# One PSUM bank for the recurrence's gradient chain, three for the scores, in a woven backward pass

## The chip, the cores and the metric

The kernel runs on one core of a Trainium2 chip. The core has five engines that run their own instruction streams in order and wait for one another through semaphores: TensorE (matmuls, PE in the profile; its weight loads are listed as PEld), VectorE (DVE), ScalarE (ACT), GpSimd (POOL) and SyncE (SP), which here issues most of the DMA transfers. Matmuls write to PSUM, which has eight banks of 2 KB per partition; a 128x512 float32 tile fills one bank. The time is that of one execution on the device, in microseconds (us); the median of five runs of the kernel before is 6302.86 us (6299.35 to 6306.31).

## What is computed

The reference computes a gated mix of two attention blocks and then all gradients of it. The output is `g * a + (1 - g) * b`; `jax.vjp` gives the gradients for eleven inputs. Cut to what matters here:

```python
def _A_ref(x, wq, wk, wv, wo):            # 32 query heads of 18, one key and value head
    q = (x @ wq).reshape(B, S, H, Dh).transpose(0, 2, 1, 3)
    k, v = x @ wk, x @ wv
    p = softmax(einsum('bhqd,bkd->bhqk', q, k) * Dh ** -0.5)
    return einsum('bhqk,bkd->bhqd', p, v) ... @ wo

def _B_ref(x, mem0, Wq, Wk, Wv, Wo, seg_len):   # 32 heads of 128
    mem = mem0                                   # 8 memory rows
    for s in range(n_seg):                       # 64 segments of 32 tokens
        h = concatenate([mem, x[:, s*32:(s+1)*32, :]], axis=1)
        q, k, v = (einsum('btd,dhe->bhte', h, W) for W in (Wq, Wk, Wv))
        p = softmax(where(mask, q k^T * scale, -1e9))
        o = einsum('bhte,hed->btd', p @ v, Wo)
        mem = o[:, :8, :]                        # the next segment needs it
        outs.append(o[:, 8:, :])
```

There are 2048 tokens of width 576. Block A is wide and has no order of its own. Block B is a recurrence: in the backward pass the gradient of a segment's eight memory rows is needed before the segment ahead of it can be done, so its 64 segments run one after another.

## The kernel before

The kernel is one program of several stages. The stage that the change touches is the backward weave. It interleaves two Python generators: `b_chain_bwd`, the chain, which carries the gradient of the memory rows from segment 63 down to 0, and `a_pass2`, the sweep, which recomputes block A's probabilities and accumulates the gradients of its keys and values. `weave` runs one piece of the chain (up to its next `yield`) and then one step of the sweep, over and over. The whole is built under a manual schedule: the instructions of an engine stand in the order in which the Python code issues them, so the order is written out by hand. Each segment has 16 pieces, and there are 64 x 16 = 1024 sweep steps.

**A sweep step n** (`a_pass2`) handles two heads for a block of 128 queries and 512 keys. On TensorE: `mm_S(n + 1)`, two score matmuls into the PSUM tile `b_S`; two matmuls into `b_dP` (a ring of three banks); four accumulating matmuls into `b_acc` for step n - 1, from `b_dS` and `b_E`. On ScalarE: `ex(n + 1)`, the exponential of `b_S` into the SBUF tile `b_E` (ring of three). On VectorE: two multiplies, `b_dS = b_dP * b_E`, one for each head. Every fourth step issues on SP the loads of `b_QD` and `b_SD` for the chunk after next (rings of three); the first step also issues `b_KV` and the first two chunks.

**A chain segment** goes through these pieces: the projection of the memory gradient `dm` by `WoT` (40 matmuls of 512 columns, `proj_part`), evacuated by ScalarE into `r_dOm`; its transposition `r_dOT` and the product `r_prod`; the gradient of the probabilities and `r_dS`; three memory gradients (`mem_grad` 2, 0 and 1), each copied by ScalarE into a part of `r_dT`, two of them after an expansion by GpSimd (`r_dSB`, `r_dSqB`); 48 units of `heads` (four matmuls of 288 columns each, against `WT`), 24 for each half of the 576 columns, each half then copied by ScalarE into `r_hs`; and `sums`, float32 matmuls that add up the heads' groups and from which VectorE writes the next `dm`. Along the way VectorE does three small transposes (`r_dsq`, `r_xq`, `r_pq`), and `load(s - 1)` issues the next segment's loads on SP: `r_vmT`, `r_vxT` (a DMA transpose), `r_pT`, `r_oT`, four `r_kx` and four `r_dx` in turn, `r_k` and `r_q`. `r_dx`, `r_k` and `r_q` are single buffers, so their loads wait for the memory gradients that read them. In the first segment `load_WT` issues six loads of `WT` on SP.

PSUM in this stage before the change: `r_pj` one bank (first half of the projection, and `heads`), `r_x` one bank (second half of the projection and all else of the chain), `b_S` two banks as one tile, `b_dP` three, `b_acc` one.

Of the kernel before, what the change touches and what calls it, by code (L numbers as in the profile page):

```python
# [6 lines left out]
ACT = mybir.ActivationFunctionType  # L7
# [3 lines left out]
F32 = mybir.dt.float32  # L11
P = 128

D = 576
NKT = 5
# [10 lines left out]
SCALEA = float(DA) ** -0.5  # L26
# [4 lines left out]
class Kern:  # L31
# [761 lines left out]
    def b_chain_bwd(self, keep, sp, psum):  # L793
        nc = self.nc
        NSEG = self.NSEG
# [9 lines left out]
        def load(s):  # L805
            L = {}
            L["vmT"] = sp.tile([P, HB, 8], BF16, name="r_vmT", bufs=2)
            nc.sync.dma_start(L["vmT"][:], self.mTd["v"][s])
            L["vxT"] = sp.tile([P, HB, 32], BF16, name="r_vxT", bufs=2)
            nc.sync.dma_start_transpose(L["vxT"][:], self.xtok["v"][s * 32:(s + 1) * 32, :])  # L810
            L["pT"] = sp.tile([P, 2, 64], BF16, name="r_pT", bufs=2)
            nc.sync.dma_start(L["pT"][:].rearrange("p a b -> p (a b)"), self.pm_dram[s])
            L["oT"] = sp.tile([P, 256], BF16, name="r_oT", bufs=2)
            nc.sync.dma_start(L["oT"][:], self.oTm_dram[s // 16][:, s % 16, :])
            L["kx"] = sp.tile([P, 8, E], BF16, name="r_kx", bufs=2)
            for c in range(4):
                nc.sync.dma_start(L["kx"][32 * c:32 * c + 32].rearrange("p u e -> p (u e)"),
                                  self.xtok["k"][s * 32:(s + 1) * 32, c * 1024:(c + 1) * 1024])
                nc.sync.dma_start(mrow["dx"][32 * c:32 * c + 8],
                                  self.dmx_dram[s * 8:s * 8 + 8, 8 * c:8 * c + 8].rearrange("m h w e -> m h (w e)"))  # L820
            for w in ("k", "q"):
                nc.sync.dma_start(mrow[w][:].rearrange("p u e -> p (u e)"), self.row_dram[w][s])
            return L
# [17 lines left out]
        for s in reversed(range(NSEG)):  # L841
            L = nxt
            d_ = dm[s % 2]
            pT = L["pT"]
            nc.gpsimd.dma_start(self.dmT_dram[:, :, s, :], d_[:, :, 0:8])
            dOm = sp.tile([P, 8, E], BF16, name="r_dOm", bufs=1)
            pj = [psum.tile([P, 512], F32, name=nm, bufs=1) for nm in ("r_pj", "r_x")]
            for k, parts in enumerate((((0, (0, 1, 2, 3)),), ((0, (4,)), (1, (0, 1))), ((1, (2, 3, 4)),))):
                for j, kts in parts:
                    self.proj_part(pj[j], d_, self.WoT, j, kts)  # L850
                    if kts[-1] == 4:
                        self.evac(dOm[:, 4 * j:4 * j + 4, :].rearrange("p u e -> p (u e)"), pj[j][:], use="s")
                if s == NSEG - 1 and k == 1:
                    self.load_WT()
                yield
            src = self.mem_T(dOm, psum, "r_x", 1)
# [29 lines left out]
            ph = {}  # L886
# [3 lines left out]
            def heads(n):  # L890
                for _ in range(n):
                    wi, hf, u = next(units)
                    if hf not in ph:
                        ph[hf] = psum.tile([P, 288], F32, name="r_pj", bufs=1)
                    for g in range(4):
                        self.mm(ph[hf][32 * g:32 * g + 32, :], lhsT=dT[:, wi, u, :],
                                rhs=self.WT[wi][:, 8 * g + u, 288 * hf:288 * hf + 288],
                                start=(wi == 2 and u == 0), stop=(wi == 1 and u == 7), tp=(0, 32 * g))
                    if wi == 1 and u == 7:
                        nc.scalar.copy(hs[:, 288 * hf:288 * hf + 288], ph[hf][:])  # L900

            def sums(kts):
                for kt in kts:
                    ncols = KT_ROWS[kt]
                    self.mm(pm[0:ncols, kt, :], lhsT=hs[:, kt * P:kt * P + ncols], rhs=self.selF[:, :])

            def mem_grad(wi, name, pairs):
                pg = psum.tile([P, 8, 32], F32, name=name, bufs=1)
                for u in range(8):
                    for n, (l, r) in enumerate(pairs):  # L910
                        self.mm(pg[:, u, :], lhsT=l[u], rhs=r[u], start=(n == 0), stop=(n == 1))
                nc.scalar.copy(dT[:, wi], pg[:])
# [6 lines left out]
            mem_grad(0, "r_x", ((rows(L["kx"]), blk(dSB)), (rows(mrow["k"]), blk(dSB, 8))))  # L919
            dSqB = sp.tile([P, 8, 4, 8], BF16, name="r_dSqB", bufs=1)  # L920
            self.expand(dSqB[:], dSq[:, 0, :, 0:8], 8)
            heads(4)
            yield
            heads(4)
            mem_grad(1, "r_x", ((rows(mrow["dx"]), [seln] * 8), (rows(mrow["q"]), blk(dSqB))))
            nc.gpsimd.dma_start(self.dTm_dram[s // 16][:, :, s % 16, :], dT[:].rearrange("p w u c -> p w (u c)"))
            if s:
                nxt = load(s - 1)
            yield
            heads(6)  # L930
            yield
            heads(6)
# [2 lines left out]
                nc.gpsimd.dma_start(self.pq_dram[s // 4, s % 4, :, c, :, 32 * (s % 4):32 * (s % 4) + 32],  # L935
                                    xq[32 * c:32 * c + 8].rearrange("p i u k -> p (i u) k"))
            yield
            heads(4)
            yield
            heads(6)  # L940
            yield
            heads(6)
            pm = psum.tile([P, NKT, 8], F32, name="r_x", bufs=1)
            sums((0, 1))
            yield
            heads(6)
            if s:
# [1 line left out]
            yield  # L949
            heads(6)  # L950
            yield
            sums((2, 3, 4))
            dn = dm[1 - s % 2]
            nc.vector.tensor_copy(dn[:, 0:4, 0:8], pm[:, 0:4, :])
            nc.vector.tensor_copy(dn[0:64, 4, 0:8], pm[0:64, 4, :])
# [554 lines left out]
    def a_pass2(self, keep, sp, psum):  # L1510
        nc = self.nc
        T, NTT = self.T, self.NTT
        KV = keep.tile([P, T], BF16, name="b_KV")
        nc.sync.dma_start(KV[:, :], self.kv_dram[:, :])
        Q, S, E_, D_ = {}, {}, {}, {}
        NC = 4 * NPR * NTT // 4

        def load(c):
            if c < NC:
                p, q4 = (c // 4) % NPR, c % 4  # L1520
                QD = sp.tile([P, 512], BF16, name="b_QD", bufs=3)
                nc.sync.dma_start(QD[:], self.qd_dram[p][:, q4 * 512:(q4 + 1) * 512])
                SD = sp.tile([P, 4, P], BF16, name="b_SD", bufs=3)
                nc.sync.dma_start(SD[:], self.sd_dram[p][:, 4 * q4:4 * q4 + 4, :])
                Q[c] = (QD, SD)

        def pair(n):
            return n // (NPR * NTT), n // 4, n % 4

        def mm_u(dst, n, base):  # L1530
            kb, c, j = pair(n)
            for i in range(2):
                r = slice(base + 32 * i, base + 32 * i + 32)
                self.mm(dst[i], lhsT=Q[c][0][r, j * P:j * P + P], rhs=KV[r, kb * 512:kb * 512 + 512],
                        tp=(base + 32 * i, 0))

        def mm_S(n):
            S[n] = psum.tile([P, 2, 512], F32, name="b_S", bufs=1)
            mm_u([S[n][:, i, :] for i in range(2)], n, 0)

        def ex(n):
            E_[n] = sp.tile([P, 2, 512], BF16, name="b_E", bufs=3)
            nc.scalar.activation(E_[n][:], S.pop(n)[:], ACT.Exp, scale=SCALEA)  # L1543

        load(0)
        load(1)
        mm_S(0)
        ex(0)
        acc = None
        NS = NPR * NTT  # L1550
        NP_ = 4 * NS
        for n in range(NP_ + 1):
            if n < NP_:
                if n % 4 == 2:
                    load(n // 4 + 2)
                if n + 1 < NP_:
                    mm_S(n + 1)
                dP = [psum.tile([P, 512], F32, name="b_dP", bufs=3) for _ in range(2)]
                mm_u([t[:] for t in dP], n, 64)
                if n + 1 < NP_:  # L1560
                    ex(n + 1)
                D_[n] = sp.tile([P, 2, 512], BF16, name="b_dS", bufs=2)
                for i in range(2):
                    nc.vector.tensor_tensor(out=D_[n][:, i, :], in0=dP[i][:], in1=E_[n][:, i, :], op=ALU.mult)  # L1564
            if n > 0:
                o = n - 1
                if o % NS == 0:
                    acc = psum.tile([P, 512], F32, name="b_acc", bufs=1)
                SD = Q[o // 4][1]
                src = (D_.pop(o), E_.pop(o))  # L1570
                for i4 in range(4):
                    self.mm(acc[32 * i4:32 * i4 + 32, :], lhsT=SD[:, o % 4, 32 * i4:32 * i4 + 32],
                            rhs=src[i4 // 2][:, i4 % 2, :],
                            start=(o % NS == 0), stop=(o % NS == NS - 1), tp=(0, 32 * i4))
                if o % NS == NS - 1:
                    dkv = sp.tile([P, 512], BF16, name="b_dkv", bufs=1)
                    nc.scalar.copy(dkv[:], acc[:])
                    k0 = (o // NS) * 512
                    nc.sync.dma_start(self.dkv_dram[:, k0:k0 + 512], dkv[:])
            yield  # L1580
# [229 lines left out]
```

The softmax here doesn't subtract the row's maximum and nothing guards it: scores larger than these inputs give would overflow.

## Time and profile before

| what | value |
|---|---|
| median of five runs | 6302.86 us |
| the profiled execution | 6302.93 us, span 6301.2 us |
| TensorE busy, share of the span | 5687.2 us, 90% |
| VectorE | 3753.6 us, 60% |
| ScalarE | 3483.2 us, 55% |
| GpSimd | 1952.0 us, 31% |
| the backward weave | first `b_S` matmul at 3198.57 us, last at 4863.90 us |

Times inside the profile are counted from the start of the span. "Busy" of an engine is the time in which at least one of its instructions runs; matmuls are pipelined, so a busy TensorE is not one at its peak. A group's line gives its source line, engine and operation, what it writes and reads, shapes and count; then its busy time and the mean duration in ns; then the idle time of the engine just before it and what ended most of that. Nearly all matmuls carry line 66, that of a helper, and are told apart by their tiles. In a timeline a line holds start, duration, engine, line, operation and count, in microseconds. The chain that ended last is followed backwards from the end of the program, from each instruction to what released it.

### The profile page before, as it was taken

The page shows a single profiled execution, that of the slowest core. Times are in us where ns is not written, and L with a number is a line of the kernel's source. Part 1 is how long each engine was busy: PE and PEld are TensorE (multiplying, and loading weights), DVE is VectorE, ACT ScalarE, POOL GpSimd, SP SyncE. Part 2 cuts the span into 40 slices and gives each one's busy share as a digit, 9 for nine tenths or more (in the row PEclk, how much of TensorE's full clock was granted, in tenths as well). Part 3 has the DMA queues.
Part 4 walks back from the last instruction along what each step waited for, and adds up shares of the span by engine and source line. Part 5 has one row for each costly group of instructions (what it writes and reads, how often), then busy time and mean ns, then how long its engine had stood idle before and what let it go on. Part 6 is the DMA issues. An engine that isn't in the chain of part 4 may idle for free.

```text
span 6301.2 us, 208815 instructions
## 1 busy us (share of the span) xinstructions
PE 5687.2 (90%) x88611; PEld 3382.1 (54%) x88822; DVE 3753.6 (60%) x7061; ACT 3483.2 (55%) x5105; POOL 1952.0 (31%) x3451
## 2 busy tenths in 40 slices
PE   7898999999999994999969999999998999899996
PEld 5443444444444443877735555555554777674443
DVE  4336777777777773666658888888887111121111
ACT  3326777777777773666647777777776222111101
POOL 3002333333333333444423333333333111122212
PEclk9999999999999997999989999999999999999998
DMA  4646666666665444999973444444343999896643
GB/s 153 227 150 114 121 120 122 122 124 120 121 123 108 99 86 140 256 258 257 257 223 108 109 112 109 107 107 107 109 108 102 248 239 244 246 259 198 221 149 113
DMA packets 1368110, 991.96 MB, mean 157 GB/s; under 512 B 931613, under 2 KB 1184806, under 8 KB 1356486
## 3 DMA queue, kind: packets, MB, share of 16 engines
q1 hardware_dynamic: 1285030, 780.53, 50.4%
q0 software_dynamic: 82144, 198.05, 10.0%
q8 instruction: 696, 11.40, 0.8%
q14 instruction: 240, 1.97, 0.1%
HBM read 552.41 MB, written 384.76 MB: 149 GB/s over the span
## 4 chain that ended last, share of the span: by engine, by line
PE 63%; ACT 18%; issue 8%; DMA 7%; SPq 3%; POOL 1%; DVE 1%; ACTq 0%; POOLq 0%; DVEq 0%
ACT b_E L1543 10%; PE w_acc L66 10%; PE c_pj L66 7%; PE a_acc L66 6%; PE b_S L66 6%; ACT a_E L1401 5%; PE a_S L66 5%; PE p_pb L66 4%; PE r_pj L66 4%; DMA dsx_dram<-x_dS 3%; PE r_x L66 2%; PE x_tr L71 2%; PE b_acc L66 2%; PE c_x L66 2%; PE y_pdx L66 2%
## 5 line engine op out<-in xcount | busy, mean ns | idle before, releaser
L1434 DVE TENSOR_TENSOR a_W<-a_dP,a_E 128x512 bf16<-128x512 f32 x2048 | 1315.6, 684 | 427.9 <-PE a_dP L66 365.6
L1564 DVE TENSOR_TENSOR b_dS<-b_dP,b_E 128x512 bf16<-128x512 f32 x2048 | 1313.2, 683 | 239.4 <-issue 120.0
L1543 ACT ACTIVATE b_E<-b_S 128x1024 bf16<-128x1024 f32 x1024 | 1047.8, 1023 | 445.5 <-PE b_dP L66 322.4
L1401 ACT ACTIVATE a_E<-a_S 128x1024 bf16<-128x1024 f32 x1024 | 1051.5, 1027 | 154.6 <-PE a_dP L66 139.4
L66 PE MATMUL b_S<-b_KV,b_QD 32*128 32x512 bf16 x2048 | 400.0, 381 | 157.0 <-ACT b_E L1543 101.3
L66 PE MATMUL r_pj<-WT,r_dT 128*32 128x288 bf16 x12288 | 492.2, 287 | 1.6 <-DMA WT<-st_WT 1.6
L66 PE MATMUL a_S<-a_QD,l_KV 32*128 32x512 bf16 x2048 | 398.6, 382 | 105.2 <-ACT a_E L1401 93.4
L66 PE MATMUL w_acc<-w_d,w_h 128*128 128x512 bf16 (+1 forms) x2352 | 470.9, 379 | 2.5
L66 PE MATMUL b_acc<-b_dS,b_SD 128*32 128x512 bf16 x2048 | 418.9, 390 | 0.4 <-DVE b_dS L1564 0.2
L66 PE MATMUL a_acc<-a_W,l_WK 128*32 128x512 bf16 x4096 | 413.4, 389 | 0.2 <-DVE a_W L1434 0.2
L66 PE MATMUL a_acc<-a_E,l_VK 128*32 128x512 bf16 x4096 | 402.9, 380 | 9.1 <-ACT a_acs L1439 0.3
L66 PE MATMUL b_acc<-b_E,b_SD 128*32 128x512 bf16 x2048 | 402.9, 390 | 0.0
L66 PE MATMUL b_dP<-b_KV,b_QD 32*128 32x512 bf16 x2048 | 399.6, 385 | 0.0
L66 PE MATMUL a_dP<-a_QD,l_KV 32*128 32x512 bf16 x2048 | 398.1, 385 | 0.0
L66 PEld LDWEIGHTS <-r_dT 128*32 128x32 bf16 x12288 | 332.2, 97 | 80.2 <-issue 2.0
L1034 DVE COPY y_T<-y_pt 128x512 bf16<-128x512 bf16 x256 | 97.0, 420 | 463.7 <-PE y_pt L71 463.7
L66 PEld LDWEIGHTS <-b_QD 32*128 32x128 bf16 x4096 | 164.4, 91 | 347.0 <-issue 283.8
L66 PEld LDWEIGHTS <-w_h 128*128 128x128 bf16 (+1 forms) x2400 | 212.9, 100 | 244.7 <-issue 3.4
L66 PEld LDWEIGHTS <-hm 128*32 128x32 bf16 x7680 | 223.1, 97 | 218.2 <-issue 34.6
L66 PEld LDWEIGHTS <-l_KV 32*128 32x128 bf16 x4096 | 135.3, 91 | 284.1 <-issue 259.5
L1020 ACT CAST y_tdk<-y_pk 128x512 bf16<-128x512 f32 x128 | 75.0, 586 | 379.0 <-PE y_pk L66 217.0
L66 PE MATMUL y_pdx<-WT,y_T 128*128 128x288 bf16 x2048 | 272.7, 287 | 0.0
(410 smaller groups left out, 11367.2 us busy)
## 6 DMA issues: line engine op xcount, KB each, us to landing
b_QD<-qd_dram SPq DMA_DIRECT2D x256, 128.0 KB
b_SD<-sd_dram SPq DMA_DIRECT2D x256, 128.0 KB
dOx_dram<-p_tok SPq DMA_DIRECT2D x16, 1024.0 KB
c_vx<-vx_dram SPq DMA_DIRECT2D x256, 64.0 KB
krow_dram<-c_k POOLq DMA_DIRECT2D x64, 256.0 KB, 2.8
qrow_dram<-c_q POOLq DMA_DIRECT2D x64, 256.0 KB, 2.6
vrow_dram<-c_v POOLq DMA_DIRECT2D x64, 256.0 KB, 4.6
x_q<-qx_dram SPq DMA_DIRECT2D x32, 512.0 KB
```

The source lines that it names most:

```text
L66: return self.nc.tensor.matmul(out, lhsT, rhs, start=start, stop=stop, tile_position=tp, skip_group_check=True)
L71: return self.nc.tensor.transpose(out, in_, self.identB[b:b + nrows, b:b + nrows], tile_position=tp)
L1020: nc.scalar.copy(d[w][:, r, :], pk[:])
L1034: nc.vector.tensor_copy(T_[t][w][:], pt[:])
L1401: nc.scalar.activation(E_[n][:], S.pop(n)[:], ACT.Exp, scale=SCALEA)
L1434: nc.vector.tensor_tensor(out=W_[n][:, i, :], in0=dP[i][:], in1=E_[n][:, i, :], op=ALU.mult)
L1543: nc.scalar.activation(E_[n][:], S.pop(n)[:], ACT.Exp, scale=SCALEA)
L1564: nc.vector.tensor_tensor(out=D_[n][:, i, :], in0=dP[i][:], in1=E_[n][:, i, :], op=ALU.mult)
```

## The change

The chain's `r_pj` tile is given up and all of the chain's PSUM tiles take turns in the one bank `r_x`. The freed bank goes to the scores: `b_S` becomes a ring of three tiles of one bank, one for each head, and `ex` issues one 128x512 exponential per head in place of one of 128x1024. The chain's 16 pieces are cut anew. The projection takes two pieces in place of three; the memory gradients 0 and 1 stand alone, without units of `heads`; the 48 units come as eight pieces of six (before: 4, 4, 6, 6, 4, 6, 6, 6, 6); the sums are issued in the last piece in place of two in one piece and three in another. With that, `load_WT` is issued in the first piece in place of the second, and `load(s - 1)` in the seventh in place of the eighth.

```diff
-            pj = [psum.tile([P, 512], F32, name=nm, bufs=1) for nm in ("r_pj", "r_x")]
-            for k, parts in enumerate((((0, (0, 1, 2, 3)),), ((0, (4,)), (1, (0, 1))), ((1, (2, 3, 4)),))):
-                for j, kts in parts:
-                    self.proj_part(pj[j], d_, self.WoT, j, kts)
-                    if kts[-1] == 4:
-                        self.evac(dOm[:, 4 * j:4 * j + 4, :].rearrange("p u e -> p (u e)"), pj[j][:], use="s")
-                if s == NSEG - 1 and k == 1:
+            for j in range(2):
+                pj = self.proj_mem(d_, self.WoT, j, psum, "r_x", 1)
+                self.evac(dOm[:, 4 * j:4 * j + 4, :].rearrange("p u e -> p (u e)"), pj[:], use="s")
+                if s == NSEG - 1 and j == 0:
                     self.load_WT()
                 yield
...
-                        ph[hf] = psum.tile([P, 288], F32, name="r_pj", bufs=1)
+                        ph[hf] = psum.tile([P, 288], F32, name="r_x", bufs=1)
...
             self.expand(dSqB[:], dSq[:, 0, :, 0:8], 8)
-            heads(4)
-            yield
-            heads(4)
+            yield
             mem_grad(1, "r_x", ((rows(mrow["dx"]), [seln] * 8), (rows(mrow["q"]), blk(dSqB))))
             nc.gpsimd.dma_start(self.dTm_dram[s // 16][:, :, s % 16, :], dT[:].rearrange("p w u c -> p w (u c)"))
             if s:
                 nxt = load(s - 1)
+            yield
+            heads(6)
             yield
             heads(6)
             yield
...
-            heads(4)
-            yield
             heads(6)
             yield
             heads(6)
-            pm = psum.tile([P, NKT, 8], F32, name="r_x", bufs=1)
-            sums((0, 1))
+            yield
+            heads(6)
             yield
             heads(6)
...
-            sums((2, 3, 4))
+            pm = psum.tile([P, NKT, 8], F32, name="r_x", bufs=1)
+            sums(range(NKT))
...
         def mm_S(n):
-            S[n] = psum.tile([P, 2, 512], F32, name="b_S", bufs=1)
-            mm_u([S[n][:, i, :] for i in range(2)], n, 0)
+            S[n] = [psum.tile([P, 512], F32, name="b_S", bufs=3) for _ in range(2)]
+            mm_u([t[:] for t in S[n]], n, 0)

         def ex(n):
             E_[n] = sp.tile([P, 2, 512], BF16, name="b_E", bufs=3)
-            nc.scalar.activation(E_[n][:], S.pop(n)[:], ACT.Exp, scale=SCALEA)
+            for i, t in enumerate(S.pop(n)):
+                nc.scalar.activation(E_[n][:, i, :], t[:], ACT.Exp, scale=SCALEA)
```

`proj_mem`, which the new code calls, allocates one tile of 128x512 and issues the same matmuls:

```python
    def proj_mem(self, st, Wt, j, psum, tag, nb):
        pj = psum.tile([P, 512], F32, name=tag, bufs=nb)
        self.proj_part(pj, st, Wt, j, range(NKT))
        return pj
```

## The prediction

> **What bounds the kernel now.** I began with the slices of the page, cut into windows: the backward weave runs from 3199 to 4866 us, TensorE busy 92% (737.53 of the 800 us from 4000), VectorE 87%, ScalarE 75%, granted clock 1.00. No engine is full, so I read the costliest groups next.
>
> ```profile
> L1564 DVE TENSOR_TENSOR b_dS<-b_dP,b_E 128x512 bf16<-128x512 f32 x2048 | 1313.2, 683 | 239.4 <-issue 120.0
> L1543 ACT ACTIVATE b_E<-b_S 128x1024 bf16<-128x1024 f32 x1024 | 1047.8, 1023 | 445.5 <-PE b_dP L66 322.4
> L66 PE MATMUL b_S<-b_KV,b_QD 32*128 32x512 bf16 x2048 | 400.0, 381 | 157.0 <-ACT b_E L1543 101.3
> ```
>
> ScalarE waits for TensorE (322.4) and TensorE's score matmul for ScalarE (101.3): a loop. The chain that ended last shows one turn of it:
>
> ```profile
> 4007.36 0.39 PE b_S L66 x2
> 4007.74 0.08 PE b_dP L66 x2
> 4007.83 0.00 issue
> 4007.83 1.03 ACT b_E L1543
> 4008.86 0.04 issue
> 4008.91 0.39 PE b_S L66 x2
> ```
>
> Scores, exp of both heads, next scores into the same two banks: 4008.91 - 4007.36 = 1.55 us, whatever else a step holds. A segment has 16 sweep steps. Over the 64 segments the medians between score matmuls are 1.55 in twelve steps, and 1.76, 1.64, 1.61, 1.93 in the four whose chain piece is too long for 1.55; sum 25.54, median segment 25.58. What a step costs TensorE when nothing holds it is read in TensorE's timeline:
>
> ```profile
> 4012.07 0.39 PE L66 MATMUL b_S<-b_KV,b_QD 32*128 32x512 bf16 x2
> 4012.08 0.39 PE L66 MATMUL b_dP<-b_KV,b_QD 32*128 32x512 bf16 x2
> 4012.40 0.39 PE L66 MATMUL b_acc<-b_dS,b_SD 128*32 128x512 bf16 x2
> 4012.41 0.39 PE L66 MATMUL b_acc<-b_E,b_SD 128*32 128x512 bf16 x2
> 4012.62 0.91 PE L66 MATMUL r_pj<-WT,r_dT 128*32 128x288 bf16 x24
> 4013.46 0.61 PE L66 MATMUL r_x<-selF,r_hs 128*128 128x8 f32 x4
> 4014.01 0.39 PE L66 MATMUL b_S<-b_KV,b_QD 32*128 32x512 bf16 x2
> ```
>
> Scores to accumulation 0.32, accumulation to chain piece 0.22 (0.33 for full-width pieces, as at 4017.44 to 4017.77), six heads 0.85, then the next scores. So a six-head step needs 0.32 + 0.22 + 0.85 = 1.39, only 0.16 under the loop.
>
> **Part 1: a ring of three and exp per head.** The second score of step n+1 now waits only for the first half of exp n. Two exps replace one:
>
> ```profile
> L623 ACT ACTIVATE x_E<-x_S 128x512 bf16<-128x512 f32 x128 | 76.4, 597 | 39.7 <-issue 18.9 <-PE x_S L66 12.2 <-DVE x_qT L61 7.2
> ```
>
> The same form exists: 0.597. Neighbours on ScalarE overlap by 0.10 (exp from 4001.32 for 1.02, the next instruction at 4002.24), so a pair takes 1.10 against 1.02: 1.28 us more per segment. ScalarE then has 16 x 1.00 + 2.6 of copies = 18.6 of some 25, off the path; without that cover it would cost 82 us. What is late next is VectorE. Accumulation n-1 waits for both multiplies of n-1:
>
> ```profile
> 4007.87 1.29 DVE L1564 TENSOR_TENSOR b_dS<-b_dP,b_E 128x512 bf16<-128x512 f32 x2 [0.26 <-issue]
> 4009.08 0.70 DVE L830 STREAM_TRANSPOSE r_xq<-r_xpad 128x512 bf16<-128x512 bf16 x1
> 4009.70 2.56 DVE L1564 TENSOR_TENSOR b_dS<-b_dP,b_E 128x512 bf16<-128x512 f32 x4
> ```
>
> The multiplies start 0.50 after their matmul (4007.36) and take 1.29; then accumulation 0.22, six heads 0.85, and two steps have passed: (0.50 + 1.29 + 0.02 + 0.22 + 0.85)/2 = 1.44 per head step, not 1.39. And the 0.70 transpose, which hid in the idle 0.26 of several steps, now pushes the multiplies late.
>
> **Part 2: the chain in one bank, 16 pieces cut anew.** No matmul is added, but the pieces are less even.
> - Sums: five column blocks in one step. Six of its matmuls took 0.82 and four 0.61, so 0.105 each; ten give 1.24, and the next scores start 0.06 before a piece ends. 0.32 + 0.33 + 1.2 + 0.2 (its fp32 weights wait for the copy r_hs, 0.39 + latencies) = 2.05.
> - Projections: 20 matmuls in five groups, 4 x 0.213 + 0.39 - 0.06 = 1.18. The first step 0.54 + 1.18 = 1.72; the second also waits for the copy r_dOm (0.585) out of the bank it needs, covered but for 0.20: 1.92. Before, these 40 matmuls lay in three steps of 1.55.
> - The five light pieces, r_dOT to the third memory gradient: TensorE needs 0.95, 1.5, 1.15, 1.15, 1.15. VectorE sets them: ten multiplies x 0.615, plus r_prod 0.29, r_dS 0.28, pad 0.17, transpose 0.45, less overlaps, 7.1; it stands idle some 0.5 on entry after the long projections. 7.6. GpSimd's expansions (1.07, 0.62) still end before their readers.
> - Eight head steps: 8 x 1.44 = 11.5. The transposes of 0.70 and 0.43 push 1.0; slack of 0.19 a step (1.44 - 1.25) takes up two thirds: 11.9.
>
> Sum 2.05 + 1.72 + 1.92 + 7.6 + 11.9 = 25.2. The same bookkeeping on the kernel before gives 25.48 where the trace has 25.58, so I add the 0.10: 25.3. Gain 0.26 (unrounded) per segment.
>
> [...] The rows: the copies out of r_x take 0.37 to 0.59, and between two pieces lie 0.54 to 0.65 of sweep matmuls. [...]
>
> **Part 3: two moved loads.** `load_WT` now runs in the first piece, before the sweep's first step, so on SP's queue the six loads of WT (2304 KB each) stand ahead of b_KV and the first b_QD; the built order confirms it. Before:
>
> ```profile
> 3193.31 0.43 SPq L1514 DMA_DIRECT2D b_KV<-kv_dram  x1
> 3193.86 0.36 SPq L1522 DMA_DIRECT2D b_QD<-qd_dram  x1
> ...
> 3195.91 3.80 SPq L791 DMA_DIRECT2D WT<-st_WT  x6
> 3199.76 0.44 SPq L1522 DMA_DIRECT2D b_QD<-qd_dram  x1
> ```
>
> The b_QD issued behind WT, at 3199.76, held TensorE until 3235.03, the ninth score matmul; eight had run by then, the first at 3198.57. After, the *first* score waits behind WT. 512 KB fewer stand ahead of it (SP's loads that each wait for one WT were issued 5.6 us apart, from 3206.53 to 3223.60, so 1.2 us): 3233.8. Ten steps at 1.58, less 0.5 for the unblocked second score, plus 1.2 for the halved matmul rate after the wait (3235.03 to 3239.33 took 4.30 for 3.1) reach the eleventh score at 3250.3, against 3239.33: 11 us lost.
>
> The other: `load(s-1)` moves from the eighth piece to the seventh, past the sweep's load of b_QD in that step. On SP that b_QD now stands behind the seven r_kx and r_dx loads, r_k and r_q; r_dx waits for the third memory gradient, and from the first r_dx to that b_QD were 4.0 us (4006.01 to 4010.05). It is issued 4.2 after the gradient and read five steps later, 1.46 + 1.42 + 1.46 + 1.42 + 1.84 = 7.6. Landing may take 3.4. No row gives it for SP; GpSimd's loads landed in 2.2 to 3.6, and the first b_QD, on busy engines, in 4.7. I take 2.5 (DMA traffic after 4010.05 had drained by 4013): free. Bounds 0 and (4.2 + 4.7 - 7.6) = 1.3 per segment.
>
> **Sum.** The eleven cover ten steps; 1014 steps, 63.4 segments, remain: 63.4 x 0.26 = 16.5 gained. 6302.93 (span 6301.2 plus 1.7; median 6302.86, so no correction) + 11 - 16.5 = 6297. That is within 0.2% (12.6 us), about what this measurement can tell from no change.
>
> **Rivals.** (A) Near no change, 6297: 0.42. Own range 6290 to 6315.
> (B) Faster: VectorE keeps ahead; the second copy wait (0.20), the transposes' 0.35 and the 0.4 of entry all hide. 0.95 x 63.4 = 60: 6237, half of it 6267. For: the loop's idle is gone on three engines. Against: at 4010.78 the accumulation already waited 0.2 for that transpose. 0.17.
> (C) Slower: b_QD lands late every segment. From 3.4 us of landing on, each 0.1 costs 6.3; at 4.0, 38 us: 6335. For: 512 KB of r_k and r_q directly ahead of it. Against: only 0.7 us of waits for b_QD in 1500 us before. 0.17.
> (D) Slower: the one bank. If ten handovers each show 0.1 more than I count, 63 us: 6360; it decides from 0.03 each. 0.14.
> (E) The start costs nothing, because b_KV's transfer slips past WT on its queue: 6286, faster by 0.26%. Against it the 35 us of the b_QD above. 0.10.
>
> Faster B + E 0.27, same 0.42, slower C + D 0.31. The range reaches halfway into B and C: 6270 to 6332.
>
> **What would show it.** Right: first score near 3234; score matmuls no longer waiting for exp; head steps 1.38 to 1.46 but one near 1.84 after the transpose; sums near 2.05; accumulation waiting for VectorE; segments near 25.3. Wrong: waits for b_QD in every segment (C), TensorE waiting for r_x copies (D), segments under 25.0 (B), a first score near 3199 (E).

## The result, and the profile after

| | before | after |
|---|---|---|
| median of all runs | 6302.63 us (6292.61 to 6310.94, 44 runs) | 6309.09 us (6298.49 to 6322.67, 26 runs) |
| ratio of after to before | | 1.0011, 95% interval 1.0006 to 1.0017 |
| first projection matmul of the weave to last `b_S` matmul | 3178.80 to 4863.90: 1685.1 us | 3170.89 to 4863.68: 1692.8 us |
| first score after that projection matmul | 19.8 us | 52.6 us |
| the 62 segments from the second on, each from its first projection matmul to the next one's | 1590.8 us, median segment 25.58 | 1589.9 us, median segment 25.54, shortest 25.25 |

The changed kernel is 0.11% slower: some 7 us (4 to 11). That lies within the forecast's 0.2% and within its range, but on the other side of before: 6297 was forecast, a gain of 6. The profiled execution of after happens to be the fastest of its 26 runs (6298.49 us). The stages ahead of the weave, which are the same in both kernels, ended 7.9 us earlier in it (3170.89 against 3178.80). Hence the weave is compared by its own length, from its first projection matmul: +7.7 us, which agrees with the +6.5 of the medians.

The page of after, its costliest groups, in the lines that answer those of before:

```profile
L1561 DVE TENSOR_TENSOR b_dS<-b_dP,b_E 128x512 bf16<-128x512 f32 x2048 | 1302.0, 681 | 231.0 <-issue 146.7
L1540 ACT ACTIVATE b_E<-b_S 128x512 bf16<-128x512 f32 x2048 | 1115.6, 599 | 325.1 <-PE b_dP L66 285.1
...
L66 PE MATMUL b_S<-b_KV,b_QD 32*128 32x512 bf16 x2048 | 411.7, 386 | 59.6 <-DMA b_QD<-qd_dram 59.0
```

The exps have doubled in number at 0.599 us each and keep ScalarE busy 1115.6 us instead of 1047.8: 68 us more on an engine that is not the bound. The score matmul no longer waits for exp (before: 157.0 idle, 101.3 of it for exp). In its place it waits 59.0 for `b_QD`. So the loop is opened, as the change meant, and a DMA has taken its place. Where these waits lie is seen in two windows of the chain that ended last. At the weave's start (start, duration, what):

```profile
3188.56 0.43 SPq L1510
3188.99 0.04 issue
3189.03 34.35 DMA b_QD<-qd_dram
3223.39 0.05 issue
3223.44 0.65 PE b_S L66 x2
```

The first `b_QD`, issued at 3189.03, held the first score until 3223.44. On SP's queue the six loads of `WT` stand right ahead of it:

```profile
3185.54 2.98 SPq L791 DMA_DIRECT2D WT<-st_WT  x6
3188.56 0.43 SPq L1510 DMA_DIRECT2D b_KV<-kv_dram  x1
3189.03 0.46 SPq L1518 DMA_DIRECT2D b_QD<-qd_dram  x1
```

That was expected. The other place was not. The same view in the middle of the weave:

```profile
4162.39 0.75 PE r_x L66 x24
4163.14 0.22 SPq L822
4163.36 0.04 issue
4163.41 4.88 DMA b_QD<-qd_dram
4168.28 0.05 issue
4168.33 0.39 PE b_S L66 x2
```

And what SP issues there:

```profile
4158.75 0.28 SPq L819 DMA_DIRECT2D r_dx<-dmx_dram  x1
...
4162.55 0.34 SPq L822 DMA_DIRECT2D r_k<-krow_dram  x1
4162.98 0.38 SPq L822 DMA_DIRECT2D r_q<-qrow_dram  x1
4163.41 0.43 SPq L1518 DMA_DIRECT2D b_QD<-qd_dram  x1
```

The first `r_dx` went out at 4158.75 and `b_QD` 4.66 us later, as the last of the row: this is the moved `load(s - 1)`. The score that reads the chunk followed 4.92 us after that issue. This is the segment with the longest wait, 1.89; in the median of the waiting segments 3.42 us pass from the first `r_dx` to `b_QD`. The waits of the stretch 3300 to 4860, without the start (who waits, for whom: us in total, times, longest), show how often:

```profile
ACT b_E L1540 <- PE b_dP L66: 271.0, 486, 2.7
...
PEld L66 <- DMA b_QD<-qd_dram: 32.1, 46, 2.2
...
PE b_S L66 <- DMA b_QD<-qd_dram: 18.2, 32, 1.9
```

32 times the score matmul waits for the chunk, in about half of the segments. (The weight load's 46 waits are partly the same moments, so the two are not added.) In the waiting segments the score came 3.4 to 5.1 us after the issue, mostly 4.2 to 5.1, with a median of 4.6; less its own wait, TensorE was ready for it 3.0 to 4.3 us after the issue. An undisturbed segment takes 25.25, which is what the new order can do; the mean over 62 segments is 25.64.

The medians between score matmuls, piece by piece, against the forecast:

| pieces | forecast | measured in after |
|---|---|---|
| projections | 1.72 + 1.92 | 1.74 + 1.95 |
| five light pieces | 7.6 | 1.04 + 2.01 + 1.31 + 1.40 + 1.74 = 7.50 |
| eight head pieces | 11.9 | 1.43, 1.52, 1.43, 1.52, 2.06, 1.39, 1.56, 1.39: 12.30, or 12.03 with the fifth as it is without `b_QD` waits (1.79) |
| sums | 2.05 | 2.02 |
| segment | 25.2, with correction 25.3 | 25.25 undisturbed |

The fifth head piece is where the late chunk is read. Its 1.79 without such waits comes from VectorE's transpose `r_xq` (0.70, from 4009.21), as TensorE's timeline of an undisturbed segment shows:

```profile
4008.89 0.39 PE L66 MATMUL b_S<-b_KV,b_QD 32*128 32x512 bf16 x2
...
4009.21 0.51 PE L66 MATMUL b_acc<-b_dS,b_SD 128*32 128x512 bf16 x2
...
4010.41 0.39 PE L66 MATMUL b_S<-b_KV,b_QD 32*128 32x512 bf16 x2
...
4010.84 0.68 PE L66 MATMUL b_acc<-b_dS,b_SD 128*32 128x512 bf16 x2
...
4012.20 0.39 PE L66 MATMUL b_S<-b_KV,b_QD 32*128 32x512 bf16 x2
```

From score to accumulation 0.32 in the first step; in the second 0.43, and the accumulation itself stretches from 0.51 to 0.68, since its second half, at 4011.14, waits for a multiply that comes late behind the transpose and ends at 4011.08 (kernel 8 below tests this). The step takes 1.79 instead of the 1.52 of its like.

### The profile page after: what moved, and what is told of

Same layout as the page of the kernel before. It is cut to its first block, busy times and chain, and to the rows that moved or that the text cites. A ratio compares the mean times of both kernels' runs of the same rounds, so it can differ in the third digit from the quotient of the medians.

```text
span 6296.7 us, 210673 instructions
## 1 busy us (share of the span) xinstructions
PE 5791.8 (92%) x88611; PEld 3428.3 (54%) x88822; DVE 3742.8 (59%) x7061; ACT 3532.2 (56%) x6129; POOL 1952.0 (31%) x3451
## 4 chain that ended last, share of the span: by engine, by line
PE 72%; DMA 9%; issue 7%; ACT 7%; SPq 2%; POOL 1%; DVE 1%; ACTq 0%; POOLq 0%; DVEq 0%
PE r_x L66 11%; PE w_acc L66 10%; PE c_pj L66 7%; PE b_acc L66 6%; PE a_acc L66 6%; ACT a_E L1397 5%; PE b_S L66 5%; PE a_S L66 5%; PE p_pb L66 4%; DMA b_QD<-qd_dram 3%; PE x_tr L71 2%; DMA dsx_dram<-x_dS 2%; PE c_x L66 2%; PE y_pdx L66 2%; PE x_b L66 1%
## 5 line engine op out<-in xcount | busy, mean ns | idle before, releaser
L1540 ACT ACTIVATE b_E<-b_S 128x512 bf16<-128x512 f32 x2048 | 1115.6, 599 | 325.1 <-PE b_dP L66 285.1
L66 PE MATMUL b_acc<-b_dS,b_SD 128*32 128x512 bf16 x2048 | 519.6, 386 | 0.4 <-DVE b_dS L1561 0.4
L66 PE MATMUL r_x<-WT,r_dT 128*32 128x288 bf16 x12288 | 512.5, 286 | 0.0
L66 PE MATMUL b_dP<-b_KV,b_QD 32*128 32x512 bf16 x2048 | 426.0, 385 | 0.0
L66 PEld LDWEIGHTS <-r_dT 128*32 128x32 bf16 x12288 | 376.3, 96 | 40.8 <-issue 0.3
L66 PEld LDWEIGHTS <-b_SD 128*32 128x32 bf16 x4096 | 161.5, 93 | 329.8 <-issue 309.5
```

The source lines that it names most:

```text
L66: return self.nc.tensor.matmul(out, lhsT, rhs, start=start, stop=stop, tile_position=tp, skip_group_check=True)
L1540: nc.scalar.activation(E_[n][:, i, :], t[:], ACT.Exp, scale=SCALEA)
```

## The experiments

The theory after these readings: the change opens the loop (a gain), loses the start to `WT`, and gives the rest back to `b_QD`, which the moved `load(s - 1)` puts behind 512 KB. Its rivals: the single bank or VectorE costs what is missing, and the `b_QD` waits only fill idle time; or the loss is all at the start. All ratios are against the kernel before on the same chip, with 95% intervals. "Weave" is the length from the first projection matmul to the last score, in the profiled execution.

| kernel | ratio | weave, us | median segment |
|---|---|---|---|
| before | | 1685.1 | 25.58 |
| after | 1.0011 (1.0006 to 1.0017) | 1692.8 | 25.54 |
| 1 after, `load(s-1)` back | 0.998 (0.997 to 0.999) | 1669.1 | 25.25 |
| 2 after, `load_WT` back | 0.9998 (0.9989 to 1.0007) | 1686.0 | 25.57 |
| 3 after, both back | 0.9961 (0.9949 to 0.9973) | 1659.5 | 25.25 |
| 4 after, old score tile and one exp | 1.0059 (1.0047 to 1.0071) | 1719.8 | 25.90 |
| 5 before, exp per head on two banks | 0.9972 (0.996 to 0.9984) | 1665.3 | 25.27 |
| 6 before, `load_WT` early | 1.0016 (1.0007 to 1.0025) | 1694.5 | 25.57 |
| 7 after, `b_QD` a chunk earlier | 0.998 (0.9971 to 0.9989) | 1669.3 | 25.25 |
| 8 as 3, transposes moved | 0.9936 (0.9923 to 0.9948) | 1638.8 | 24.90 |
| 9 as 3, two score banks | 0.999 (0.9981 to 0.9999) | 1676.3 | 25.52 |
| 10 as 5, transposes moved | 0.9956 (0.9943 to 0.9968) | 1649.7 | 25.05 |
| 11 after, only `r_k`, `r_q` behind `b_QD` | 0.9964 (0.995 to 0.9977) | 1669.0 | 25.25 |

**1. The segment's loads moved back by one piece.**

```diff
-            if s:
-                nxt = load(s - 1)
             yield
             heads(6)
+            if s:
+                nxt = load(s - 1)
             yield
```

> The changed kernel with the next segment's loads issued one piece later again, after the first six heads, so that the sweep's b_QD stands ahead of them on SP's queue. Queue theory: the waits for b_QD go (32 us of weight loads waiting in the changed kernel's trace), segments fall from a mean of 25.67 to the floor of 25.3, 0.37 x 63 = 23 us: near 6286 against 6309 for the changed kernel and 6303 before. Rival, the one bank costs the time: b_QD waits were only where a late TensorE happened to stand, and the time stays near 6309.

Measured: the weave is 23.7 us shorter than in after (1669.1 against 1692.8), every segment is at 25.25, and the step after the transpose is 1.79. The same entry of the waits, 3300 to 4860:

```profile
PEld L66 <- DMA b_QD<-qd_dram: 2.5, 11, 0.2
```

32.1 us have become 2.5, and the score matmul's own 18.2 are gone from the list. The `b_QD` waits are on the path: with what follows from them they cost 23.7 us, 0.37 for each of 64 segments.

**2 and 3. `load_WT` back in the second piece, alone and with 1.**

```diff
-                if s == NSEG - 1 and j == 0:
+                if s == NSEG - 1 and j == 1:
                     self.load_WT()
```

> The changed kernel with load_WT in the second piece again, behind the sweep's first loads. Start theory: the eleventh score matmul came 8.9 us later, counted from the first projection matmul, so 9 us return: near 6300. Rival, the start was hidden or lost to something else: 6309. In the trace the first score should come some 20 us after the first projection matmul, not 52.

> Both loads back where they were; what stays is the ring of three, exp per head and the one bank. If the two costs are separate they add: 6309 - 23 - 9 = 6277, some 0.4% under the kernel before. If one of them covers the other, 6285 to 6300.

Measured: with `WT` back the first score stands 19.5 us after the projection, as before, and the weave shrinks by 6.8 us on top of after, and by 9.6 on top of kernel 1 (1669.1 to 1659.5). The `b_QD` waits stay in kernel 2 (35.3 us on the weight load, 21.5 on the score) and go in kernel 3. So the two losses lie in different places and nearly add: taken back alone they give 23.7 and 6.8, together 33.3. Less the 25.6 by which kernel 3 beats before, that is the +7.7 of after.

**4. One bank for the chain and the new pieces, without the ring of three and the exp per head.**

```diff
-            S[n] = [psum.tile([P, 512], F32, name="b_S", bufs=3) for _ in range(2)]
-            mm_u([t[:] for t in S[n]], n, 0)
+            S[n] = psum.tile([P, 2, 512], F32, name="b_S", bufs=1)
+            mm_u([S[n][:, i, :] for i in range(2)], n, 0)
...
-            for i, t in enumerate(S.pop(n)):
-                nc.scalar.activation(E_[n][:, i, :], t[:], ACT.Exp, scale=SCALEA)
+            nc.scalar.activation(E_[n][:], S.pop(n)[:], ACT.Exp, scale=SCALEA)
```

> The changed kernel with the scores as before: one tile of two banks, one exp of 128x1024, one bank left unused. Only the chain's one bank, the recut pieces and the moved loads remain. By the step bookkeeping the recut pieces in the old 1.55 us loop need 25.9 per segment against 25.5: +26 us, and the start +9: near 6338, more if b_QD is late here too. If one bank and recut pieces cost nothing: 6312.

Measured: 25.90 per segment against 25.58 before: the single bank and the new pieces together cost 0.32 a segment when the loop is still closed. (`b_QD` is late here too, 4.9 us of waits on the score, and the start is that of after; so the weave is 34.7 us longer than before.) In the chain of waits, 4000 to 4012, a full-width piece is followed by a copy and then by the closed loop:

```profile
4006.01 1.28 PE r_x L66 x20
4007.29 0.02 issue
4007.32 0.32 ACT r_dOm L63
4007.64 0.16 issue
4007.80 1.04 ACT b_E L1539
4008.84 0.04 issue
4008.88 0.39 PE b_S L66 x2
```

The copy of the second projection half holds the exp in ScalarE's order, the exp holds the next scores: 0.51 us from the end of the matmuls to the start of the exp. The cost shows here as a copy ahead of an exp, behind a piece that is longer than any of the old projection's. How much of the 0.32 is the bank's is not shown, as no run has the new pieces on two banks; the expectation had put 25.9 down to the pieces alone. Between two pieces the chain has 0.66 of sweep matmuls (4003.58 to 4004.24 in the same chain of waits), where the copies out of `r_x` took 0.37 to 0.59 in before. That these matmuls cover most of the copies is the author's estimate; no run takes them away.

**5. Exp per head alone, on the two old banks.** The old kernel keeps `r_pj` and its old pieces; its score tile of two banks becomes a ring of two tiles of one bank.

```diff
-            S[n] = psum.tile([P, 2, 512], F32, name="b_S", bufs=1)
-            mm_u([S[n][:, i, :] for i in range(2)], n, 0)
+            S[n] = [psum.tile([P, 512], F32, name="b_S", bufs=2) for _ in range(2)]
+            mm_u([t[:] for t in S[n]], n, 0)
...
-            nc.scalar.activation(E_[n][:], S.pop(n)[:], ACT.Exp, scale=SCALEA)
+            for i, t in enumerate(S.pop(n)):
+                nc.scalar.activation(E_[n][:, i, :], t[:], ACT.Exp, scale=SCALEA)
```

> The kernel before with one thing changed: the scores are two tiles of one bank and each head has its own exp; the chain keeps its two banks and its pieces, no bank is added. If exp per head brings the gain and the third bank is not needed, segments fall to about 25.0 and the time to 0.995 of before. By the step bookkeeping the second score still waits for the second exp, which now ends 0.08 us later, and light steps gain what long ones lose: 25.57 against 25.48, 6 us, 1.001 of before.

Measured: 25.27 a segment and a ratio of 0.9972, between the two expectations and met by neither. The gain, 0.31 a segment, needs no third bank: the first score tile is free after the first exp, so TensorE starts on head 0 of the next step while ScalarE still works on head 1. One such place, from ScalarE's and TensorE's timelines:

```profile
4009.09 1.09 ACT L1544 ACTIVATE b_E<-b_S 128x512 bf16<-128x512 f32 x2 [0.45 <-PE b_dP L66]
4009.99 0.60 PE L66 MATMUL b_S<-b_KV,b_QD 32*128 32x512 bf16 x2
```

The pair of exps ends at 4010.18, the next scores begin at 4009.99.

**6. `load_WT` early in the old kernel.**

```diff
-                if s == NSEG - 1 and k == 1:
+                if s == NSEG - 1 and k == 0:
                     self.load_WT()
```

> The kernel before with load_WT one piece earlier, nothing else. Start theory: the sweep's first scores wait behind WT, 9 to 11 us lost, 1.0015 to 1.0017 of before, the first score some 50 us after the first projection matmul in place of 20. Rival, the cost of the start belongs to the ring or the pieces: 1.000.

Measured: first score 52.9 us after the projection (before 19.8, after 52.6), weave +9.4 us, ratio 1.0016. The price of the start is the same from both sides: 9.4 added to before, 9.6 taken from kernel 1.

**7. `b_QD` and `b_SD` a chunk earlier.** Rings of four, the loads issued four steps sooner (a third chunk is loaded at the start), all else as in after.

```diff
-                QD = sp.tile([P, 512], BF16, name="b_QD", bufs=3)
+                QD = sp.tile([P, 512], BF16, name="b_QD", bufs=4)
...
-                SD = sp.tile([P, 4, P], BF16, name="b_SD", bufs=3)
+                SD = sp.tile([P, 4, P], BF16, name="b_SD", bufs=4)
...
-                    load(n // 4 + 2)
+                    load(n // 4 + 3)
```

> The changed kernel with rings of four for b_QD and b_SD, each loaded one chunk (four steps) earlier; load(s-1) and load_WT stay where the change put them. If the lateness of b_QD behind load(s-1) is the cost, it goes as it did when load(s-1) was moved back: 20 us, 0.998 of before. If load(s-1) itself, earlier, cost something else (its transfers collide with others), the time stays at 1.001.

Measured: 25.25 a segment, weave 1669.3, as in kernel 1 (1669.1). The order of the loads is that of after, only the slack is larger: it is the chunk's lateness that costs, not the traffic of the moved loads.

**11. Only `r_k` and `r_q` behind `b_QD`.** `load(s - 1)` stays in the seventh piece with `r_kx` and `r_dx`; the two last loads, 512 KB, get a function of their own.

```diff
             heads(6)
+            if s:
+                load_kq(s - 1)
             yield
```

> The changed kernel with r_k and r_q (2 x 256 KB) taken out of load(s-1) and issued one piece later, behind the sweep's b_QD; the r_kx and r_dx loads stay ahead of it. If the 512 KB directly ahead make b_QD late, it is issued 0.9 us earlier and lands 1.2 us earlier still (512 KB at the 2304 KB in 5.6 us of the WT loads), more than all but the longest waits: 0.998 of before, as with load(s-1) moved back whole. If it is the small packets of r_kx and r_dx, or waiting for r_dx, most of the waits stay: 1.000 to 1.001.

Measured: 25.25 a segment, weave 1669.0, no wait for `b_QD` in the list of waits. SP's queue in one segment:

```profile
4152.15 0.33 SPq L819 DMA_DIRECT2D r_dx<-dmx_dram  x1
4152.52 0.34 SPq L1523 DMA_DIRECT2D b_QD<-qd_dram  x1
4152.90 0.43 SPq L1525 DMA_DIRECT2D b_SD<-sd_dram  x1
4153.38 0.43 SPq L825 DMA_DIRECT2D r_k<-krow_dram  x1
4153.91 0.38 SPq L825 DMA_DIRECT2D r_q<-qrow_dram  x1
```

`b_QD` follows the last `r_dx` at once, and `r_k` and `r_q` come after it. So without the two loads directly ahead of `b_QD` the chunk is in time, though the seven `r_kx` and `r_dx` still stand before it. These seven take most of its slack, the two the rest: from issue to score the chunk has 11.6 us in kernel 1 and 5.1 here (medians). The issue of `r_k` and `r_q` alone puts `b_QD` back by 0.86 us (4162.55 to 4163.41 in after). Of the score's 32 waits in after 29 are shorter than that, and three are longer (0.91, 1.25 and 1.89), so their transfer can have a part in it. The run takes both away together and doesn't part them. Its ratio, 0.9964, is lower than the 0.998 of kernel 1 although the weaves are equal to 0.1 us; the two intervals overlap, and a difference, if there is one, does not lie in the weave.

**9. Two score banks with the new pieces**, `bufs=2` in place of 3, else as kernel 3.

> The kernel e3_both_back (one bank for the chain, recut pieces, both loads back) with two score banks in place of three, one of the eight left unused; exp stays per head. e5_exp_per_head fell to 25.27 per segment without a third bank. If exp per head is all that frees the loop, this stays at 25.25 and 0.996 of before. If the third bank works on the recut pieces, the second score waits for the second exp again: 25.74 by the step bookkeeping (which was 0.3 too high for e5_exp_per_head, so 25.4 to 25.75), 10 to 31 us over e3_both_back, 0.9977 to 1.001.

Measured: 25.52. With 4 (25.90) and 3 (25.25) this gives the account of a segment on the new pieces: one bank and new pieces +0.32 (from 25.58), exp per head -0.38, the third bank -0.27. Kernel 5, which changes neither bank nor pieces, is at 25.27. From there the chain's single bank and the new pieces cost 0.25 (25.52), and the third bank brings 0.27 back: it no more than pays for them.

**8 and 10. The transposes out of the way.** In 8, built on kernel 3, `r_xq` is transposed behind the sums, its four stores go out in the next segment's seventh piece, and `r_pq` is transposed in the last head piece, its pad copied one piece ahead. In 10, built on kernel 5, `r_xq` is transposed in the 13th piece, behind the first sums, and the pad of `r_pq` copied there.

```diff
             heads(6)
-            xq = to_q((pT[:, 0, :], dS[:, 0, :]), "x", nc.gpsimd)
-            for c in range(4):
-                nc.gpsimd.dma_start(self.pq_dram[s // 4, s % 4, :, c, :, 32 * (s % 4):32 * (s % 4) + 32],
-                                    xq[32 * c:32 * c + 8].rearrange("p i u k -> p (i u) k"))
+            to_pad((pT[:, 0, :], dS[:, 0, :]), "x", nc.gpsimd)
...
             nc.vector.tensor_copy(dn[0:64, 4, 0:8], pm[0:64, 4, :])
+            held = (s, to_q((0, 0), "x", None))
```

> Both loads back as in e3_both_back, and VectorE's transposes of 0.70 and 0.43 us moved out of the short head steps: the first behind the sums, ahead of the long projections (its four stores follow in the next segment's seventh piece), the second into the last head piece. If VectorE sets the head steps, the 0.35 per segment booked for the transposes returns: segments 24.9, 22 us under e3_both_back, 0.9926 of before. If TensorE alone sets them: 25.25 and 0.996 as e3_both_back.

> The kernel e5_exp_per_head (chain in two banks and in its old pieces, two score banks, exp per head) with VectorE's transposes of 0.70 and 0.43 us moved: the first from the tenth piece to the thirteenth, where heads and sums hold TensorE for 1.9 us, the second with its pad copied one piece earlier. If VectorE sets these steps here too, 0.25 to 0.35 per segment goes, 24.95, 0.994 of before, level with e8_transposes_moved without the change's single bank. If the old pieces are bound by ScalarE's pair of exps: 25.27, 0.997.

Measured: kernel 8 takes 24.90 a segment, 0.35 below kernel 3, which is what the prediction had put on the transposes. It ran 6257.96 us where before ran 6302.8: ratio 0.9936, the best of all, 0.6% faster than before, and 0.75% faster than after (0.9936/1.0011). Kernel 10 gains 0.22 of 25.27, a little less than the 0.25 to 0.35 expected, and ends at 0.9956. The two place the work differently, so 24.90 against 25.05 is not the worth of the third bank alone.

## Why the prediction was right or wrong

Its sum was +11 - 16.5 + 0 against before. The runs give, on the weave's length:

| term | forecast | measured | by |
|---|---|---|---|
| loop opened, new pieces | -16.5 | -25.6 | 3 against before |
| `WT` ahead of the first `b_QD` | +11 | +9.6 (6: +9.4) | 1 against 3 |
| `b_QD` behind `load(s-1)` | 0 (bounds 0 and 1.3 a segment) | +23.7, 0.37 a segment | after against 1 |
| sum | -5.5 | +7.7 | after against before |

**The step that failed** is the last of Part 3: "Landing may take 3.4 ... I take 2.5 ...: free." The slack was not at fault. TensorE was ready 3.0 to 4.3 us after the issue, in 21 of the 32 waiting segments 4.0 or more, since mostly 3.4 us passed from the first `r_dx` to `b_QD` and not the 4.0 read in before. The landing was mis-sized: in the waiting segments the score came 3.4 to 5.1 after the issue, with a median of 4.6, as long as `r_k` and `r_q` go ahead (kernel 11).

The 2.5 was read from how soon the core's DMA traffic had fallen after a `b_QD` in the same place of SP's queue in before (4010.05 to 4013). That traffic, summed over 16 engines, doesn't tell when this one load was complete, and in before the chunk behind these loads was read four steps later (8.4 us after its issue in the median, against 4.2 in after), so that no wait could show it. Of the other rows named, the 2.2 to 3.6 of GpSimd are the medians of stores (`dOm_dram`, `pq_dram`) and not of loads; the 4.7 of the first `b_QD` was the near one, and it went into the bound alone. The bounds were 0 and 1.3 a segment, and the truth, 0.37, lies between; but the sum took the 0; with 0.37 in its place it would have forecast a loss (-5.5 + 23.7, some 18 us).

This is rival C's mechanism, with its argument "512 KB of r_k and r_q directly ahead of it", in half of the segments rather than in all. Its counterargument, few waits for `b_QD` before, was read where the chunk had those four steps more, and says nothing of the new order.

**Right in kind, too small: the loop.** Predicted -0.26 a segment; the figures as printed give 25.58 - 25.19 - 0.10 = 0.29, which is 18 us and not 16.5. The groups of pieces are right to 0.13, and an undisturbed segment takes 25.25 where 25.2 was summed and 25.3 taken. The 0.10 added because the same bookkeeping fell 0.10 short on before was not needed; that it had to do with the closed loop, which is gone, is likely but not shown. The rest is the base: before was taken at its median segment, 25.58, while its mean is 25.66 (1590.8/62); kernel 3's mean is 25.26. That is 0.394 x 62 = 24.4 of the 25.6.

**Right: the start,** 11 forecast, 9.6 and 9.4 measured; the first score came at 3223.44 in a run whose projection began 7.9 us earlier, 52.6 us behind it, where the forecast of 3233.8 was 55.0 behind 3178.80. Rival E, a start for nothing, falls.

**Right: VectorE is next.** The head steps alternate at 1.43 and 1.52 (forecast 1.44 with the excess of the transposes spread), and the transpose's 0.35 is shown by kernel 8. Rival B, in which that hides, falls in after; kernel 8 gets its 0.35 by moving the work, not by hiding it.

**Rival D** falls as stated: 0.1 for each of ten handovers would be 1.0 a segment. The single bank and the new pieces together cost 0.32 behind the closed loop (kernel 4) and 0.25 with exp per head on two banks (9 against 5); with the third bank the steps are within the pieces' forecast.

One thing that the prediction did not ask: whether the exp per head needed the freed bank. It argued the two as one part. Kernel 5 shows that nearly all of the segment's gain (0.31 of 0.33) is had by splitting the tile that was already there, without a new order of pieces and without the two moved loads that cost 33 us.

## What to carry to other kernels

When a change moves a group of loads past another load on the same queue, look up who reads that load and how many microseconds of slack it has left with the bytes now ahead of it; a duration read from the old order did not hold here (2.5 taken, 4.6 from issue to score measured). A tile of two banks with one reader can be made into a ring by splitting the reader, before any bank is taken from elsewhere (kernel 5: 25.58 to 25.27 a segment). And when several edits go together, take the cheapest one out by itself: here that one alone beat the whole (0.9972 against 1.0011).

## What the hardware showed that was not expected

One wait cost a second time. After the 1.89 us in which TensorE waited for `b_QD`, its matmuls ran slower from some point after 4168.88 until 4172.66 (TensorE's timeline; in brackets the idle time before and its releaser):

```profile
4168.33 0.39 PE L66 MATMUL b_S<-b_KV,b_QD 32*128 32x512 bf16 x2 [1.89 <-DMA b_QD<-qd_dram]
...
4168.88 1.31 PE L66 MATMUL r_x<-WT,r_dT 128*32 128x288 bf16 x24
4170.12 0.60 PE L66 MATMUL b_S<-b_KV,b_QD 32*128 32x512 bf16 x2
...
4171.06 1.66 PE L66 MATMUL r_x<-WT,r_dT 128*32 128x288 bf16 x24
4172.66 0.39 PE L66 MATMUL b_S<-b_KV,b_QD 32*128 32x512 bf16 x2
```

The scores take 0.60 instead of 0.39, and six heads 1.66 instead of 0.91. The windows of that place show it as the clock (length; busy time and count of PE, PEld, DVE, ACT and POOL; granted clock; DMA share; GB/s):

```profile
4160.00:4164.00 4.00, 4.00 (x93) 2.50 (x89) 3.62 (x6) 2.87 (x7) 0.63 (x3) 1.00 0.52 157
4164.00:4168.00 4.00, 2.44 (x55) 1.31 (x43) 2.45 (x5) 1.96 (x5) 2.67 (x5) 1.00 0.80 228
4168.00:4172.00 4.00, 3.67 (x56) 1.77 (x60) 2.40 (x4) 2.17 (x4) 0.00 (x0) 0.66 0.15 48
4172.00:4176.00 4.00, 4.00 (x63) 2.33 (x54) 3.11 (x6) 2.47 (x5) 0.62 (x1) 0.92 0.13 37
```

The granted clock is 1.00 up to and during the wait, 0.66 after it and 0.92 in the next window: the clock falls when the work has already come back. That segment took 28.59 us, 3.3 more than an undisturbed one, for 1.89 of wait. It is the only fall of the clock among the 32 waits. A wait of 1.25 us, at 3885, was not followed by slower matmuls (0.39 for its scores), and neither was one of 1.61 in kernel 2, where the granted clock stays at 1.00:

```profile
4674.34 0.39 PE L66 MATMUL b_S<-b_KV,b_QD 32*128 32x512 bf16 x2 [1.61 <-DMA b_QD<-qd_dram]
...
4676.00:4680.00 4.00, 4.00 (x77) 2.43 (x73) 3.80 (x8) 3.36 (x7) 0.62 (x1) 1.00 0.21 66
```

So the wait of 1.25 cost about its own length (its segment took 26.58, 1.33 more than an undisturbed one) and the wait of 1.89 almost twice its own. One case does not make a border; whether the length alone decides, no run here shows.
